# A three-stage transformer-like kernel: the lead-in's order of work rewritten, the third tile's scans and scores sooner, and a buffer of its own for the second tile's scores

## The chip, the cores and the metric

The kernel runs on one core of one Trainium2 chip. The metric is the device time of one execution in microseconds (us). The engines are called as the profile calls them: PE (TensorE matmuls; PEld its weight loads), DVE (VectorE), ACT (ScalarE), POOL (GpSimd) and SP (SyncE, which here only issues DMAs).

## The reference

Three stages follow each other. The first is a linear attention with a per-channel decay w over 4 batches, 8 heads of 48 channels and 768 positions:

```python
for t in range(S):
    cur = einsum('bhd,bhe->bhde', u[None] * kt, vt)
    y[:, :, t] = einsum('bhd,bhde->bhe', rt, state + cur)
    state = wt[:, :, :, None] * state + einsum('bhd,bhe->bhde', kt, vt)
```

The second is a dense layer pair on the 3072 tokens of 384 channels, with 2048 hidden units and a leaky slope alpha for each; the third sends each token to the one of 8 experts whose embedding it is nearest to:

```python
h = x @ w_in
x = (np.maximum(h, 0.0) + alpha * np.minimum(h, 0.0)) @ w_out
...
logits = normed(x) @ normed(expert_emb).T / tau
expert_idx = np.argmax(logits, axis=1)
out[mask] = gate_w[mask, None] * (np.maximum(x[mask] @ w1[e], 0.0) @ w2[e])
```

## The kernel before, in words

**Tiles and blocks.** The attention is cut into 24 tiles n of 128 tokens (six chunks of time by four batches); three tiles make a block j of the dense layers, and there are 8 blocks. The dense weights come in sixteen chunks, eight of w_in and eight of w_out in turn, each of 256 hidden units: SP loads a chunk into one of four staging buffers `stg` (`load_stage`, L185 and L187), and `conv` turns it into two single-precision parts in four steps c0 to c3: c0 on ACT (L196), c1 on DVE (L198 and L199, two instructions), c2 on ACT, which rounds the high part (L210, `win0h`, `wout0h`), c3 on DVE, which subtracts it for the low part (L212, `win0l`, `wout0l`). A chunk's c3 releases the staging buffer for the load four chunks on. The converted weights stay for all blocks, so chunks are converted only during the first block.

**The steps of a tile**, numbered as in the table of functions `ATT`: a0 `att_p0` (the first scan over w on DVE, L261, with L263 to L267), a1 `att_p1` (the second scan, L270), a2 `att_p2` (k transposed, copied by ACT at L322), a3 `att_p3` (the scores `a_ps`, L331, copied into `A` by ACT at L334 and masked there by two POOL selects, L335), a4 `att_p4` (the tile's result `y_ps`, L365, added to `dv` by DVE at L367), a5 `att_p5` (`y` transposed on PE and split into `xh` on ACT at L382 and `xl` on DVE at L383: what the dense layers read), a6 `att_r` (r and k scaled by the scans' result: on DVE at L286), a7 `att_d` (the diagonal term: `dg` L302, and `dv`, either by eight ACT copies at L305 or by one DVE product at L307), a8 `att_w` (L276 on ACT, the sums of the decays), a9 `att_s` (the state: `u_ps` L344, `st` L350). The state of a tile enters the results of the next chunk of time, four tiles on.

**The dense steps.** `l1(j, f)` computes one 128-unit slice f of block j's hidden layer: nine products of 384 columns into `h_ps` (L407), then ACT (L411) and DVE (L412) form the activation `m`; `l1_hi` and `l1_lo` split it (`gh` L421 on ACT, `gl` L426 on DVE). `l2(j, f)` adds the slice's nine products to the block's output `o_ps` (L436). `warm(n)` issues n idle products (L391) whose result nobody reads.

**What sets the order.** Each engine runs its instructions in the order in which the program issues them. The opening is the string `PLAN` (L78): "aQ.N" is step Q of tile N, "cQ.C" step Q of the conversion of chunk C, "l1.f" the slice f of block 0, "wN" N warm products, "p0.G" and "p1.G" a small product of an output-weight chunk with the expert embeddings, "s" and "e" those embeddings' norm (L890, L891) and transpose (L887), "g" the split of all waiting `m`. Behind it a loop over T issues, for each T: the attention steps 2 to 5 that are due, an early group of conversion steps, one slice of `l1`, the slice of `l2` two T back, a late group, the attention steps 0, 1, 6 and 8, and `l1_lo`. A tile's due times are a start (`START`, `AT1`, `AT`) plus lags (`LAGS`). A tile's load is issued once the steps that read the same buffer two tiles back are issued.

Where the diff speaks: `AD` (tiles n < AD form `dv` on ACT), `AT1` (starts of the tiles of blocks 1 and 2 within their block), the one buffer `A` of all tiles' scores, the pool `ps_a` from which `y_ps` is taken (three buffers, shared with `a_ps`, `kt_ps`, `u_ps` and `ep`), and the dictionary `sched` of the due steps.

## Time and profile before

| | us |
|---|---|
| median of 3 runs | 821.88 |
| lowest, highest | 821.51, 823.42 |
| the profiled execution: its own time | 818.76 |
| its span | 816.9 |
| PE busy in the span | 793.8 (97%) |
| DVE busy | 582.0 (71%) |
| ACT busy | 435.2 (53%) |
| POOL busy | 300.9 (37%) |

The profile cuts the span into 40 slices of 20.4 us. PE's slices, in tenths: 8 in the first slice, 8, 7 and 9 in the next ones (warm products among them), and 9 (90% or more) to the end but for two of 8 and the last of 7. The granted TensorE clock is full in all slices but the third (6 tenths of full speed, 40.8 to 61.3 us). Places in the trace are given in us from the span's start. The opening of `PLAN` takes the first 52 us or so; conversions on DVE and ACT go on until about 112 us; behind that the dense layers and the attention's tiles share the engines until the routed experts begin.

How to read it: a row of a timeline has the start, the duration, the engine, the line, the operation, and its operands; in brackets at the end is the time for which the engine had waited just before and what released it. Durations of neighbouring instructions of one engine overlap a little, so where a stretch is measured, start to start is meant.

### The profile page before, as it was taken

How to read it: one execution, taken by the hardware profiler on the slowest of the kernel's cores; microseconds unless marked ns; L12 is line 12 of the kernel's file. 1: busy time of each engine (PE TensorE's matmuls, PEld its weight loads, DVE VectorE, ACT ScalarE, POOL GpSimd, SP SyncE). 2: the span in 40 equal slices, each digit the busy share in tenths (PEclk: the TensorE clock that was granted, in tenths of full speed). 3: DMA queues.
4: the chain of work that ended last, by engine and by line, in shares of the span. 5: the costliest groups of instructions: out<-in, count | busy, mean ns of one | idle time of the engine just before them, and what ended most of it. 6: DMA issues, size and time to landing. Idle time of an engine off the chain costs nothing. (4 is left out here: it accounts for less than half of the span.)

```text
span 816.9 us, 16480 instructions
## 1 busy us (share of the span) xinstructions
PE 793.8 (97%) x6466; PEld 755.7 (93%) x6466; DVE 582.0 (71%) x1229; ACT 435.2 (53%) x861; POOL 300.9 (37%) x365
## 2 busy tenths in 40 slices
PE   8879999999999999999999999998999999999997
PEld 5669899999999999999999999898899999999997
DVE  7788967886686586676676774647987676767672
ACT  6667655435345435444534533436556676767662
POOL 2002222333223134124224212143466776767731
PEclk9969999999999999999999999999999999999999
DMA  9545520133424313113113100046756787686750
GB/s 322 167 156 197 183 75 2 69 118 117 156 84 139 131 33 102 66 63 99 69 70 98 69 1 31 31 169 205 193 198 211 273 278 254 218 285 211 263 187 33
DMA packets 31623, 114.86 MB, mean 141 GB/s; under 512 B 5756, under 2 KB 13148, under 8 KB 29232
## 3 DMA queue, kind: packets, MB, share of 16 engines
q0 software_dynamic: 13952, 59.86, 22.3%
q1 hardware_dynamic: 17584, 53.85, 19.5%
q8 instruction: 53, 0.87, 0.5%
q14 instruction: 34, 0.28, 0.2%
HBM read 99.36 MB, written 15.51 MB: 141 GB/s over the span
## 5 line engine op out<-in xcount | busy, mean ns | idle before, releaser
L411 ACT ACTIVATE m<-h_ps,al_sb 128x384 f32<-128x384 f32 x128 | 74.3, 581 | 139.4 <-PE h_ps L407 137.7
L412 DVE TENSOR_TENSOR m<-h_ps,m 128x384 f32<-128x384 f32 x128 | 71.0, 555 | 97.3 <-ACT m L411 96.6
L421 ACT ACTIVATE gh<-m 128x384 fp32r<-128x384 f32 x128 | 67.1, 525 | 111.1 <-DVE m L412 111.1
L335 POOL TENSOR_SCALAR_AFFINE_SELECT A<-A 128x512 f32<-128x512 f32 x48 | 32.9, 710 | 208.1 <-ACT A L334 208.1
L426 DVE TENSOR_TENSOR gl<-m,gh 128x384 fp32r<-128x384 f32 x128 | 81.3, 636 | 38.2 <-ACT gh L421 38.0
L689 POOL DMA_INDIRECT raw<-in_w,wix x64 | 67.4, 1054 | 48.6 <-DVE w0l L701 21.3
L731 PE MATMUL h_ps<-yh,w0h 128*128 128x256 f32 x264 | 77.4, 293 | 3.4 <-DVE g2l L736 3.4
L731 PE MATMUL h_ps<-yl,w0h 128*128 128x256 f32 x264 | 75.0, 284 | 0.3 <-DVE yl L722 0.3
L731 PE MATMUL h_ps<-yh,w0l 128*128 128x256 f32 x264 | 74.7, 283 | 0.0
L701 DVE TENSOR_TENSOR w1l<-raw,w1h 128x768 fp32r<-128x768 f32 x64 | 60.6, 953 | 19.8 <-ACT w1h L700 19.1
L407 PE MATMUL h_ps<-xh,win0h 128*128 128x384 f32 x192 | 69.2, 360 | 2.3 <-DVE m L412 1.5
L701 DVE TENSOR_TENSOR w0l<-raw,w0h 128x768 fp32r<-128x768 f32 x64 | 60.8, 959 | 12.5 <-ACT w0h L700 12.5
L407 PE MATMUL h_ps<-xh,win1h 128*128 128x384 f32 x192 | 68.0, 354 | 0.0
L436 PE MATMUL o_ps<-wout0h,gh 128*128 128x392 f32 x192 | 66.7, 347 | 0.0
L407 PE MATMUL h_ps<-xh,win0l 128*128 128x384 f32 x192 | 65.4, 341 | 1.1 <-DVE win0l L212 1.1
L436 PE MATMUL o_ps<-wout0l,gh 128*128 128x392 f32 x192 | 65.9, 343 | 0.0
L436 PE MATMUL o_ps<-wout0h,gl 128*128 128x392 f32 x192 | 65.9, 343 | 0.0
L436 PE MATMUL o_ps<-wout1h,gh 128*128 128x392 f32 x192 | 65.8, 343 | 0.0
L407 PE MATMUL h_ps<-xl,win0h 128*128 128x384 f32 x192 | 65.5, 341 | 0.1
L436 PE MATMUL o_ps<-wout1h,gl 128*128 128x392 f32 x192 | 65.3, 340 | 0.0
L436 PE MATMUL o_ps<-wout1l,gh 128*128 128x392 f32 x192 | 65.2, 340 | 0.0
L407 PE MATMUL h_ps<-xh,win1l 128*128 128x384 f32 x192 | 64.9, 338 | 0.0
(282 smaller groups left out, 2261.8 us busy)
## 6 DMA issues: line engine op xcount, KB each, us to landing
ld<-in_att SPq DMA_DIRECT2D x18, 1348.5 KB, 5.8
stg<-in_w_in SPq DMA_DIRECT2D x24, 256.0 KB, 3.9
stg<-in_w_out SPq DMA_DIRECT2D x8, 768.0 KB, 4.2
x2d<-rows SPq DMA_DIRECT2D x24, 194.0 KB, 7.3
out<-zero SPq DMA_DIRECT2D x24, 192.0 KB, 6.5
ld<-in_att SPq DMA_DIRECT2D x5, 512.0 KB, 5.2
ld<-in_att SPq DMA_DIRECT2D x3, 452.5 KB, 4.6
raw<-in_w,wix POOLq DMA_INDIRECT x64, 6.1
```

The costliest lines, as they stand in the source:

```text
L335: POOL.affine_select(out=h, in_=h, pattern=[[0, HP], [1, CH]], compare_op=ALU.is_gt, fill=0.0, base=0, channel_multiplier=-1)
L407: PE.matmul(out=h, lhsT=w[:, k, :], rhs=x[:, k, :], start=(n == 0), stop=(n == 3 * KD - 1))
L411: ACT.activation(out=m, in_=h, func=AF.Copy, scale=al_sb[:, f:f + 1])
L412: DVE.tensor_tensor(out=m, in0=h, in1=m, op=ALU.min)
L421: ACT.activation(out=gh, in_=m_t[j, f], func=AF.Copy)
L426: DVE.tensor_tensor(out=gl, in0=m_t.pop((j, f)), in1=gh.bitcast(F32), op=ALU.subtract)
L436: PE.matmul(out=o_t[j][i], lhsT=g[:, s], rhs=w, start=(f == 0 and n == 0), stop=(f == KF - 1 and n == 2))
L689: POOL.indirect_dma_start(out=t, out_offset=None, in_=src, in_offset=idx(wix[:, h, COL[s]:COL[s] + 1]))
L701: DVE.tensor_tensor(out=lo, in0=a, in1=hi.bitcast(F32), op=ALU.subtract)
L731: PE.matmul(out=h, lhsT=w[:, k, :], rhs=x[:, k, :], start=(n == 0), stop=(n == 3 * KD - 1))
```

## The change

`PLAN` is another string. Tile 2's scans and its `att_r` (a0.2, a1.2, a6.2) stand right behind tile 1's, ahead of a4.0; a3.1 and a3.2 stand sooner; l1.0 is preceded by fewer steps of chunk 1 (c2.1, c3.1 and the rest now follow it); "s", "e", a2.1, p0.0 stand behind l1.0; l2.0 and l2.1 are in the plan, the second as the last main product; the warm products in it are 11 where they were 38 (the 28 that open the program are left). Tile 1's scores get a buffer `A1` in the pool `rows`; `y_ps` of tiles 0 to 2 comes from `ps_o`. Tiles 3, 4 and 5 form `dv` on ACT. Tile 3 starts 2 T later, tile 4 1 T later, tile 5 as before. On SP, the load of chunk 4 stands now ahead of tile 3's load, where it stood behind, and tile 5's load stands behind ten chunk loads where it stood behind eight. Lines of the kernel behind L324 stand 3 to 6 later: L331 is now L334, L334 is L337, L365 is L369, L367 is L371, L382 and L383 are L386 and L387, L407 is L411, L411 is L415, L412 is L416, L426 is L430, L436 is L440.

```diff
--- before.py
+++ after.py
@@ -60,7 +60,7 @@
 STEP8 = 2
 HOLD = [1, 2, 1]
 ND = range(6)
-AD = 2
+AD = (0, 1, 3, 4, 5)
 WARM0 = 28
 WPD = (2, 3)
 EARLY = [(0, 0, -2), (0, 1, -2), (0, 2, -1), (0, 3, -1), (1, 0, 0), (1, 1, 0)]
@@ -75,9 +75,9 @@
 LAGS = [0, 1, 4, 4, 6, 7, 2]
 
 LOADS = [(0, "w"), (0, "rk"), "id", "v", (0, "n"), "e", (1, "w"), (1, "rk"), (1, "n"), (2, "w"), (2, "rk"), (2, "n"), 0, 1, 2, 3, "u"]
-PLAN = "a0.0 a1.0 a8.0 a2.0 w6 a6.0 a3.0 a7.0 w8 a0.1 a1.1 a6.1 s a4.0 a3.1 a9.0 a2.1 e c0.0 a7.1 a9.1 w8 a0.2 c0.1 c0.2 a1.2 a6.2 c1.0 a4.1 w8 a3.2 c1.1 a7.2 a5.0 a5.1 c2.0 w4 a4.2 p0.0 c3.0 a5.2 c2.1 c1.2 l1.0 c3.1 c2.2 l1.1 p1.0 c0.3 c3.2 g l1.2 w4 a8.1 a2.2 a9.2"
-
-AT1 = [0, 4, 8]
+PLAN = "a0.0 a1.0 a8.0 a2.0 w6 a6.0 a3.0 a7.0 a0.1 a1.1 a6.1 w5 a3.1 a0.2 a1.2 a6.2 a4.0 c0.0 a7.1 a4.1 a3.2 c1.0 c0.1 a7.2 a5.0 a5.1 c2.0 a4.2 c3.0 a5.2 a9.0 s c1.1 c0.2 l1.0 a2.1 c2.1 g p0.0 c3.1 e c1.2 l1.1 p1.0 c0.3 c2.2 g c3.2 l2.0 c1.3 l1.2 l2.1 a9.1"
+
+AT1 = {1: [2, 5, 8], 2: [0, 4, 8]}
 AT = {2: [-1, 6], 3: [-4, 1, 7]}
 NSG = 4
 WP = 1536
@@ -134,7 +134,7 @@
     R, P = (PS[:, HP * CW * i:HP * CW * (i + 1)].rearrange("p (h t) -> p h t", h=HP)[:, :, 2:CW] for i in range(2))
     R1 = PS[:, 3:3 + HP * CW].rearrange("p (h t) -> p h t", h=HP)[:, :, 0:CH]
     anew = cp.tile([128, LW], BF16, name="anew")
-    A = atp.tile([128, H, CH], F32, tag="at", name="A")
+    A0 = atp.tile([128, H, CH], F32, tag="at", name="A")
     st_all = atp.tile([128, B, HP, D], F32, tag="st", name="st")
     st = [st_all[:, b] for b in range(B)]
     sbd_all = atp.tile([128, 2, HP, 2 * D], F32, tag="st", name="sbd")
@@ -300,7 +300,7 @@
             v = nat(n, 2).rearrange("p (h d) -> p h d", h=H)
             dg = sp.tile([128, H, 1], F32, tag="dg", name="dg")
             ACT.activation(out=dg, in_=dp, func=AF.Copy)
-            if n < AD:
+            if n in AD:
                 for h in range(H):
                     ACT.activation(out=dv[:, h, :], in_=v[:, h, :], func=AF.Copy, scale=dg[:, h, :])
             else:
@@ -321,8 +321,11 @@
                 PE.transpose(kt[:, h, :], k[:, h, :], ident)
             ACT.activation(out=Kt, in_=kt, func=AF.Copy)
 
+    A_t = {}
+
     def att_p3(n):
 
+        A = A_t[n] = rp.tile([128, H, CH], F32, tag="rows", name="A1") if n == 1 else A0
         r, k = rT(n, 0), rT(n, 1)
         a = [ps_a.tile([128, HP, CH], F32, tag="a", name="a_ps") for _ in range(2)]
         for h in range(HP):
@@ -352,9 +355,10 @@
     def att_p4(n):
         c, b = divmod(n, B)
         r, v = rT(n, 0), nat(n, 2)
+        A = A_t.pop(n)
         if 0 < c < NCH - 1:
             att_s(n)
-        yp = ps_a.tile([128, DM], F32, tag="a", name="y_ps")
+        yp = ps_o.tile([128, DM], F32, tag="o", name="y_ps") if n < BT else ps_a.tile([128, DM], F32, tag="a", name="y_ps")
 
         for hp in range(HP):
             for q in (slice(0, 64), slice(64, 128)):
@@ -850,17 +854,19 @@
         sched = {}
         for n in range(NTILE):
             j = max(q for q in range(NB) if B0[q] <= n)
-            t0 = START[n] if j == 0 else 16 * (j - 1) + (AT1 if j < 3 else AT[BLK[j]])[n - B0[j]]
+            t0 = START[n] if j == 0 else 16 * (j - 1) + (AT1[j] if j < 3 else AT[BLK[j]])[n - B0[j]]
             for q, d in enumerate(LAGS0 if j == 0 else LAGS1 if j == 1 else LAGS):
                 sched.setdefault(t0 + d, []).append((q, n))
-            sched.setdefault(1 if n == 2 else t0 + 3, []).append((8, n))
+            sched.setdefault({1: 0, 2: 1}.get(n, t0 + 3), []).append((8, n))
+        sched.setdefault(1, []).append((2, 2))
+        sched.setdefault(2, []).append((9, 2))
 
         ran = set()
 
         def run(kind, *a):
             if (kind, *a) in ran:
                 return
-            if kind != "w":
+            if kind not in "wg":
                 ran.add((kind, *a))
             if kind == "a":
                 q, n = a
@@ -976,7 +982,7 @@
                     q = (T - 2) // 16
                     bg.append(chain(route(q), *((early_table(), early_loads()) if q == NB - 2 else (last_table(),) if q == NB - 1 else ())))
             convs(T, 1)
-            pieces(T, (0, 1, 6, 8))
+            pieces(T, (0, 1, 6, 8, 9))
             if j and (j, f) in m_t:
                 l1_lo(j, f)
             step(STEP7 if j >= NB - 1 else 1)
```

**DVE in the opening.** `att_129` holds tile 2's decays, `ld` a loaded tile's; `y` is a finished tile, `en_192` the embeddings' norm. Before, from the last step of tile 1 on:

```order
L286 TENSOR_TENSOR ld<-ld,PS 128x512
L890 TENSOR_SCALAR en_192<-en_192 8x1
L891 RECIPROCAL en_192<-en_192 8x1
L367 TENSOR_TENSOR y<-y_ps,dv 128x384
L261 SCALAR_TENSOR_TENSOR PS<-att_129,anew 128x520
L263 TENSOR_SCALAR ip_all<-PS 128x4
```

With the change, from the same place:

```order
L286 TENSOR_TENSOR ld<-ld,PS 128x512
L261 SCALAR_TENSOR_TENSOR PS<-att_129,anew 128x520
L263 TENSOR_SCALAR ip_all<-PS 128x4
L264 RECIPROCAL att_129<-ip_all 128x4
L266 TENSOR_TENSOR att_129<-att_129 128x512
L267 TENSOR_TENSOR att_129<-att_129,PS 128x512
L270 SCALAR_TENSOR_TENSOR PS<-att_129,anew 128x519
L286 TENSOR_TENSOR att_129<-att_129,PS 128x512
L371 TENSOR_TENSOR y<-y_ps,dv 128x384 x2
L198 SCALAR_TENSOR_TENSOR stg<-stg 128x768
L199 SCALAR_TENSOR_TENSOR stg<-stg 128x768
L307 TENSOR_TENSOR dv<-att_129,dg 128x384
```

Tile 2's seven steps follow tile 1's without a step between; the norm and the sum of tile 0's result, which stood ahead of them, come behind, and tile 0's and tile 1's sums follow each other.

**ACT in the opening.** `dv_403` and `dv_377` are the diagonal term of tile 1, `dg` its factors, `A_125` the shared buffer of scores, `A1_330` the new one. Before, with what each waits for:

```order
L196 ACTIVATE stg_163<-stg_163 128x768 [waits DMAHW6_49,DMAHW5_49,DMAHW4_49]
L302 ACTIVATE dg_404<-dg_ps_398 128x8 [waits PE_49]
L305 ACTIVATE dv_403<-ld_156,dg_404 128x48 [waits DMAHW0_49,DVE_49,Activation_49]
L305 ACTIVATE dv_403<-ld_156,dg_404 128x48 x7
L350 ACTIVATE st_126<-u_ps_414 48x192 [waits PE_49]
L350 ACTIVATE st_126<-u_ps_414 48x192
L196 ACTIVATE stg_167<-stg_167 128x768 [waits DMAHW7_49]
L196 ACTIVATE stg_169<-stg_169 128x768 [waits DMAHW2_49,DMAHW1_49,DMAHW0_49]
L334 ACTIVATE A_125<-a_ps_487 128x512 [waits PE_49,Pool_49]
L334 ACTIVATE A_125<-a_ps_488 128x512 [waits PE_49,Pool_49]
```

With the change:

```order
L337 ACTIVATE A1_330<-a_ps_331 128x512 [waits PE_49]
L337 ACTIVATE A1_330<-a_ps_332 128x512 [waits PE_49]
L196 ACTIVATE stg_163<-stg_163 128x768 [waits DMAHW6_49,DMAHW5_49,DMAHW4_49]
L302 ACTIVATE dg_378<-dg_ps_372 128x8 [waits PE_49]
L305 ACTIVATE dv_377<-ld_156,dg_378 128x48 [waits DMAHW0_49,DVE_49,Activation_49]
L305 ACTIVATE dv_377<-ld_156,dg_378 128x48 x7
L337 ACTIVATE A_125<-a_ps_407 128x512 [waits PE_49,Pool_49]
L337 ACTIVATE A_125<-a_ps_408 128x512 [waits PE_49,Pool_49]
```

Tile 1's scores are copied into their own buffer without a wait for POOL; the eight copies of tile 1's `dv`, whose first one waits for a DMA and for DVE as before, stand ahead of the copies of tile 2's scores.

**DVE around tile 5's first scan**, in the main loop; the line of `y` is tile 3's result, whose step also releases the buffer that tile 5's load fills; the scan is tile 5's. Before, two pieces, eight rows apart:

```order
L367 TENSOR_TENSOR y<-y_ps,dv 128x384
L198 SCALAR_TENSOR_TENSOR stg<-stg 128x768
L199 SCALAR_TENSOR_TENSOR stg<-stg 128x768
L412 TENSOR_TENSOR m<-h_ps,m 128x384
L212 SCALAR_TENSOR_TENSOR win1l<-stg,win1h 128x3x256
```

```order
L426 TENSOR_TENSOR gl<-m,gh 128x384
L198 SCALAR_TENSOR_TENSOR stg<-stg 128x768
L199 SCALAR_TENSOR_TENSOR stg<-stg 128x768
L412 TENSOR_TENSOR m<-h_ps,m 128x384
L212 SCALAR_TENSOR_TENSOR win1l<-stg,win1h 128x3x256
L261 SCALAR_TENSOR_TENSOR PS<-ld,anew 128x520
L263 TENSOR_SCALAR ip_all<-PS 128x4
```

With the change:

```order
L286 TENSOR_TENSOR ld<-ld,PS 128x512
L430 TENSOR_TENSOR gl<-m,gh 128x384
L371 TENSOR_TENSOR y<-y_ps,dv 128x384
L198 SCALAR_TENSOR_TENSOR stg<-stg 128x768
L199 SCALAR_TENSOR_TENSOR stg<-stg 128x768
L416 TENSOR_TENSOR m<-h_ps,m 128x384
L212 SCALAR_TENSOR_TENSOR win1l<-stg,win1h 128x3x256
L261 SCALAR_TENSOR_TENSOR PS<-ld,anew 128x520
L263 TENSOR_SCALAR ip_all<-PS 128x4
```

The scan stood 18 rows behind the sum of tile 3's result and stands 5 rows behind it; tile 5's `dv` (L307) is no longer on DVE.

## Rows read from the trace of the kernel before

**Rows 1.** The page's first part: busy time, share of the span, instructions.

```profile
PE 793.8 (97%) x6466; PEld 755.7 (93%) x6466; DVE 582.0 (71%) x1229; ACT 435.2 (53%) x861; POOL 300.9 (37%) x365
```

**Rows 2.** Windows: length, busy of PE, PEld, DVE, ACT, POOL; clock, DMA share, GB/s.

```profile
45.00:50.00 5.00, 3.00 (x56) 2.58 (x57) 4.83 (x9) 3.30 (x6) 0.00 (x0) 0.50 0.05 21
...
80.00:90.00 10.00, 10.00 (x125) 9.18 (x126) 9.19 (x14) 8.54 (x19) 2.56 (x3) 1.00 0.44 138
```

**Rows 3.** DVE's timeline from 60 to 130 us.

```profile
64.33 0.56 DVE L412 TENSOR_TENSOR m<-h_ps,m 128x384 f32<-128x384 f32 x1 [2.14 <-ACT m L411]
...
86.39 0.56 DVE L412 TENSOR_TENSOR m<-h_ps,m 128x384 f32<-128x384 f32 x1 [0.64 <-ACT m L411]
...
111.03 0.56 DVE L412 TENSOR_TENSOR m<-h_ps,m 128x384 f32<-128x384 f32 x1 [0.80 <-ACT m L411]
```

**Rows 4.** PE's timeline from 28 to 53 us.

```profile
28.72 1.14 PE L365 MATMUL y_ps<-att,A 128*64 128x48 f32 x32
...
31.88 0.44 PE L407 MATMUL h_ps<-xh,win0h 128*128 128x384 f32 x1 [0.78 <-ACT xh L382]
...
33.98 0.34 PE L407 MATMUL h_ps<-xh,win0h 128*128 128x384 f32 x1
...
35.66 0.59 PE L243 MATMUL wq_ps<-enT,wt 128*32 128x8 f32 x48
...
46.17 1.55 PE L232 MATMUL wt_ps<-ident,stg 128*128 128x128 f32 x6 [3.77 <-DVE stg L199]
...
49.37 0.70 PE L436 MATMUL o_ps<-wout0h,gh 128*128 128x392 f32 x1
...
52.48 0.85 PE L298 MATMUL dg_ps<-u_bd,ld 128*128 128x2 f32 x4
```

**Rows 5.** DVE's timeline in the opening: tile 1's, then tile 2's first and last step.

```profile
8.54 1.23 DVE L261 TENSOR_TENSOR_SCAN PS<-ld,anew 128x520 f32<-128x520 f32 x1
...
12.67 0.94 DVE L286 TENSOR_TENSOR ld<-ld,PS 128x512 f32<-128x512 f32 x1
...
15.78 1.23 DVE L261 TENSOR_TENSOR_SCAN PS<-att,anew 128x520 f32<-128x520 f32 x1
...
20.71 0.69 DVE L286 TENSOR_TENSOR att<-att,PS 128x512 f32<-128x512 f32 x1
```

**Rows 6.** ACT's timeline in the opening: tile 1's `dv`, tile 2's scores.

```profile
19.60 1.91 ACT L305 ACTIVATE dv<-ld,dg 128x48 f32<-128x48 f32 x8
...
26.40 1.09 ACT L334 ACTIVATE A<-a_ps 128x512 f32<-128x512 f32 x2 [2.58 <-PE a_ps L331]
```

**Rows 7.** DVE's timeline, 45 to 56 us: tile 3's scans and chunk 4.

```profile
46.03 1.24 DVE L261 TENSOR_TENSOR_SCAN PS<-ld,anew 128x520 f32<-128x520 f32 x1
...
48.91 0.95 DVE L198 SCALAR_TENSOR_TENSOR stg<-stg 128x768 int32<-128x768 int32 x1
...
51.64 1.23 DVE L270 TENSOR_TENSOR_SCAN PS<-ld,anew 128x519 f32<-128x519 f32 x1
...
54.63 0.95 DVE L212 SCALAR_TENSOR_TENSOR win0l<-stg,win0h 128x768 fp32r<-128x768 f32 x1
```

**Rows 8.** DVE's timeline, 73 to 79 us.

```profile
73.80 0.55 DVE L367 TENSOR_TENSOR y<-y_ps,dv 128x384 f32<-128x384 f32 x1
...
77.51 1.00 DVE L286 TENSOR_TENSOR ld<-ld,PS 128x512 f32<-128x512 f32 x1
78.43 0.55 DVE L307 TENSOR_TENSOR dv<-ld,dg 128x384 f32<-128x384 f32 x1
78.90 0.55 DVE L426 TENSOR_TENSOR gl<-m,gh 128x384 fp32r<-128x384 f32 x1
```

**Rows 9.** The page's part on DMA issues: count, size, us to landing.

```profile
ld<-in_att SPq DMA_DIRECT2D x5, 512.0 KB, 5.2
```

**Rows 10.** Windows of PE alone: length, busy; clock, DMA share, GB/s.

```profile
19.00:20.00 1.00, 1.00 (x19) 0.76 1.02 352
...
57.00:58.00 1.00, 1.00 (x9) 0.97 0.97 340
```

## The prediction

> **What bounds the kernel now.** The page's first part comes first: PE is busy for 97% of the span, no other engine for more than 71% [rows 1]. Behind the opening the kernel is therefore as long as PE's work, and what a change of the opening can give is the time at which PE's full stretch begins, plus what PE idles for in between. Next come the windows: from 45 to 50 us PE is busy for 3.00 of 5.00 us at half clock while DVE is busy for 4.83; from 80 to 90 us PE is full, but DVE is busy for 9.19 of 10 and ACT for 8.54 [rows 2]. The timeline of DVE shows what this means: between 60 us and the last conversion, just behind 111 us, DVE waits only three times for the activation of a dense product, 2.14, 0.64 and 0.80 us [rows 3]. So from 45 to about 112 us the conversion of the weights on DVE sets the pace; PE is handed a product when its converted weights are there, and its high busy share means that it is just able to follow. Last, PE's timeline of the opening: tile 2's result y2 starts at 28.72, the first main product l1.0 at 31.88, there is an idle stretch of 3.77 before 46.17 for a conversion on DVE, and l2.0 starts at 49.37 [rows 4].
>
> The reader is to take from this two different questions: how much sooner the first main product starts, and how much of that survives until DVE has done its list. The second decides.
>
> **How much sooner l1.0 starts.** Tile 1's seven steps on DVE last from 8.54 to 12.67 + 0.94 = 13.61, that is 5.07; tile 2's, the same seven, from 15.78 to 20.71 + 0.69 = 21.40, that is 5.62 [rows 5]. With the change they start at 13.61 and end, by the one or the other length, between 18.7 and 19.2; I take 19.0. The sum of tile 0's result follows on DVE (0.55 [rows 8]), to 19.5. Now ACT: the eight copies of tile 1's dv stand ahead of the copy of tile 2's scores, and the first of them waits for DVE; I read that wait as one for tile 0's sum, because dv's buffer is in use until then. The copies last 1.91 [rows 6], to 21.4. From the start of the scores' copy (26.40) to y2 (28.72) it was 2.32 [rows 4, 6]: y2 starts at 23.7, not 28.72. From y2 to l1.0 it was 3.16 at a mostly full clock [rows 4]; at half clock a third more is the most that I allow, 4.2. So l1.0 starts between 26.9 and 27.9 against 31.88: 4.0 to 4.9 us sooner, 4.4 taken.
>
> The tile's own buffer for scores does little of this. The copy of tile 1's scores no longer waits for tile 0's masked scores, but tile 2's copy, the one that y2 needs, stands behind dv anyway.
>
> **What survives.** I keep a ledger for DVE, the engine that sets the pace, up to the end of chunk 4's conversion (54.63 before [rows 7]).
>
> 1. *The lead, 4.4 at l1.0.* Some of it is lost at half clock: nine products took 1.68 us at full clock (33.98 to 35.66) and 3.11 at half (49.37 to 52.48) [rows 4], 1.43 more. If the clock comes back during the first products, one group's half is lost at most; I take a loss of 0.6, and the lead that reaches chunk 4 is 3.8 (bounds 2.6 and 4.9).
> 2. *Tile 3's scans, not yet done there.* Tile 3 starts two T later. Its first scan with the three steps behind it stood ahead of that place on DVE and took 46.03 to 48.91, 2.88; its second scan 51.64 to 52.78 in DVE's queue, about 1.15 [rows 7]. DVE still owes 4.0. Lead and debt together: +0.2 (bounds -0.9 and +1.4).
> 3. *Three products dv (tiles 3, 4, 5) leave DVE.* Start to start one takes 78.43 to 78.90, 0.47 [rows 8]: -1.4. They come back on ACT as 1.91 each [rows 6]; with ACT busy for 3.30 of 5 us from 45 to 50 [rows 2] I price that at nothing while DVE is the later of the two. If ACT's spare time is gone, it costs what the fourth case below says.
> 4. *The three waits of before* [rows 3], 3.6 in all, are in DVE's time of before and not forced by its list: -3.6 if PE is ahead by two groups, which l2.0 and l2.1 done in the opening give it.
> 5. *A new wait on DVE for tile 5's load.* Tile 5's first scan now stands five rows behind the sum of tile 3's result, whose step releases the load's buffer, and not eighteen. Those rows (the sum, two of a conversion, m, and the low part) took 73.80 to 77.51, 3.7 [rows 8]; the load lands 5.2 behind its issue [rows 9]. DVE waits for 1.5, and everything behind the scan on DVE with it: the l1 activations and the next conversions. Bounds: 0 if the release comes before the sum is through, 5.2 if nothing lies beside it. Taken +1.5.
> 6. *PE catches up.* DVE's list is now shorter by 5.0 (points 3 and 4), PE's is not, so some of the waits for products come back before 112 us: between 0 and the 3.6 of before; nearer the upper half, since PE was busy for all of 80 to 90 us [rows 2]. Taken +2.0.
>
> SP's order costs nothing by itself: the load of chunk 4 is now ahead of tile 3's, and tile 3 has two T more. Twenty-seven warm products fewer free no time, as PE waits wherever they stood; they matter through the clock only. The second accumulator pool for y0 to y2, and the norm of the embeddings standing later, are not on the path: their readers are the wprime products, which also come later.
>
> Sum: 0.2 - 1.4 - 3.6 + 1.5 + 2.0 = **-1.3 us**. Behind 112 us the instructions are the same, so that is the whole change. The profiled execution took 818.76 with a span of 816.9, 3.1 below the median of 821.88; the durations come from it, and only the difference is used: 821.88 - 1.3 = **820.6**. With the larger unknowns (points 1, 5, 6) not all on one side, the case's own range is 819.0 to 822.6. About 0.3%, or 2.5 us, is the least that a measurement of this kernel can tell from no change: 819.4 to 824.3 counts as the same.
>
> **The rivals.**
>
> *The clock stays full in the opening (faster).* Before, PE's granted clock fell in the window 19:20 (0.76) and was back in 57:58 (0.97), with l1.0 and l1.1 in between at full speed [rows 4, 10]. If the earlier scans keep PE fed from 19 us on, nothing of the lead is lost (4.9 against a debt of 4.0: -0.9 in place of +0.2), and PE, ahead by more, gives back only 0.8 of point 6: 820.6 - 1.1 - 1.2 = 818.3. Against it: the clock fell with 14 warm products ahead of it in the plan that the change takes out in part.
>
> *The clock stays at half through l2.1 (about the same).* Then l1.0 starts at 27.9, one to two groups of products cost 1.43 more [rows 4] on the way to chunk 4, and the lead that survives is 1.1 to 2.6, against the 3.8 that I took: +1.2 to +2.7, middle +2.0, which gives 822.6. For it speaks the fall at 19.5 [rows 10] and that fewer warm products follow. The Trainium skill, in "TensorE: Matmul & The Clock Gate", section "Part 1: The HAM clock gate (the "warmup" mystery)", says that "the default state is throttled, and activity releases the throttle"; by that rule a change which takes idle products away does so at the price of the clock, and the time would be this rival's 822.6. The trace agrees in part: the clock fell at 19 us, though warm products stood ahead.
>
> *DVE is not what sets the pace (faster).* If PE's products are what DVE's three waits show, and the rest only looks tight, a first product that starts 4.4 sooner is kept, less half a microsecond: 817.9. Against it: in 51 us DVE waits for a product for 3.6 [rows 3].
>
> *ACT becomes the bound (slower).* Three times eight copies, 1.91 each [rows 6], are put on ACT between T = 4 and T = 9, about 60 to 90 us, where it is busy for 8.54 of 10 us [rows 2]; each time gh and the next activation m stand behind the copies, and DVE and PE wait for these. The price is 5.7 less the 1.5 that is free there, 4.2: 820.6 + 4.2 = 824.8. It decides once ACT has no more than 1.9 us free in a T in which a dv stands ahead of m. For it: 8.54 of 10. Against it: from 90 us on, ACT's work per T must fall, for DVE is the busier of the two over the whole span [rows 1].
>
> *The change doesn't do what it says* in part: tile 2's scans come 2 us sooner, but the order on ACT (dv ahead of the scores) makes l1.0 wait, and nothing but the waits moves. That is 821.9; I count it with the first case, in whose range it lies.
>
> **How the numbers follow.** The forecast's case (DVE's list sets the pace and swallows the lead): 0.50. Clock full: 0.18. Clock at half: 0.13. ACT the bound: 0.10. DVE not the pace: 0.09. Faster than 819.4 are most of the second (0.15), the last (0.09) and the lower end of the first (0.06): 0.30. Slower than 824.3 are most of ACT's case (0.09) and what is left over of the half clock and of a late load of tile 5 (0.04): 0.13. The same: 0.57. The range leaves out the lower half of the two faster cases, 0.10, and most of ACT's, 0.10: 817.9 to 823.6.
>
> **What would show it.** In the changed kernel's profile tile 2's last step on DVE should end near 19, y2 start near 23.7 and l1.0 between 27 and 28. L212 of chunk 4 should end within 1 us of 54.6 less the 4.0 of tile 3's scans, and the last conversion near 111. If L261 of tile 5 waits for a DMA by more than 3 us, or an activation on ACT stands behind dv while DVE is idle, the fourth case or a late load is at work. If PE's granted clock from 27 to 42 us is full, the second case holds; if it is 0.5, the third. The prediction is wrong in its core if the last conversion ends 4 us sooner than before: then DVE's list did not swallow the lead.

## The result, and the profile after

The changed kernel takes 826.46 us (median of 5 runs, 825.88 to 826.62) against 821.88 of the kernel before measured beside it (5 runs): 1.0052 times, 95% interval [1.0037, 1.0067]. It is slower, by 4.6 us; the forecast was 820.6 in a range of 817.9 to 823.6. The profiled execution of the changed kernel took 826.46 with a span of 824.4, that of before 818.76 with 816.9; of these 7.5 us of span about 3 arise before 115 us, which this part is about, and the rest behind 550 us, which the last section takes up.

The page's first part, to be held against [rows 1]: no engine has more work, PE's is spread over a longer span.

```profile
PE 793.0 (96%) x6439; PEld 757.4 (92%) x6439; DVE 581.7 (71%) x1226; ACT 439.5 (53%) x885; POOL 301.2 (37%) x365
```

PE's clock in the opening: length and busy time of PE, then the granted clock, DMA share and GB/s.

```profile
19.00:26.00 7.00, 6.28 (x46) 0.54 0.38 129
26.00:32.00 6.00, 5.25 (x49) 0.50 0.31 77
32.00:38.00 6.00, 5.46 (x75) 0.90 0.66 228
```

The granted clock lies at half (its lower level, 1.2 GHz) from about 20 to 33 us, right where the first main products now run. PE's timeline of the opening answers to [rows 4]:

```profile
24.87 2.22 PE L369 MATMUL y_ps<-att,A 128*64 128x48 f32 x32
...
28.65 0.88 PE L347 MATMUL u_ps<-ld,Kt 128*48 128x48 f32 x16
29.46 0.69 PE L411 MATMUL h_ps<-xh,win0h 128*128 128x384 f32 x1
...
34.48 0.44 PE L411 MATMUL h_ps<-xh,win0h 128*128 128x384 f32 x1
...
39.65 0.44 PE L411 MATMUL h_ps<-xh,win0h 128*128 128x384 f32 x1 [0.16 <-ACT win0h L210]
...
50.63 0.89 PE L243 MATMUL wq_ps<-enT,wt 128*32 128x8 f32 x48 [4.20 <-ACT wt L234]
...
52.26 0.69 PE L411 MATMUL h_ps<-xh,win0h 128*128 128x384 f32 x1
```

Tile 2's result y2 starts at 24.87 (28.72 before), the first main product l1.0 at 29.46 (31.88): 2.4 us sooner, not 4.4. In front of l1.0 a state product u_ps has moved in. The next slices are not sooner: l1.1 starts at 34.48 (33.98 before) and l1.2 at 39.65, where the kernel before had

```profile
36.22 0.41 PE L407 MATMUL h_ps<-xh,win0h 128*128 128x384 f32 x1
```

Then PE idles 4.20 us before 50.63, for ACT, in the place of the 3.77 for DVE of before. The next rows are DVE's, to be held against [rows 3, 7]:

```profile
46.41 0.56 DVE L430 TENSOR_TENSOR gl<-m,gh 128x384 fp32r<-128x384 f32 x1 [2.17 <-ACT gh L425]
...
52.41 0.96 DVE L212 SCALAR_TENSOR_TENSOR win0l<-stg,win0h 128x768 fp32r<-128x768 f32 x1 [0.25 <-ACT win0h L210]
...
87.61 1.24 DVE L261 TENSOR_TENSOR_SCAN PS<-ld,anew 128x520 f32<-128x520 f32 x1 [2.27 <-DMA ld<-in_att]
...
110.14 0.56 DVE L416 TENSOR_TENSOR m<-h_ps,m 128x384 f32<-128x384 f32 x1 [1.46 <-ACT m L415]
...
113.98 0.56 DVE L416 TENSOR_TENSOR m<-h_ps,m 128x384 f32<-128x384 f32 x1 [1.95 <-ACT m L415]
114.46 0.95 DVE L212 SCALAR_TENSOR_TENSOR wout1l<-stg,wout1h 128x768 fp32r<-128x768 f32 x1
```

Chunk 4's low part (52.41, first line of L212) comes 2.2 us sooner than before (54.63), with tile 3's scans still to do. The runs below show that these 2.2 us are not the opening's. Later DVE waits 2.27 for tile 5's load, and twice for an activation, 1.46 and 1.95. The last conversion starts at 114.46; in the kernel before it started at 111.51. From there on the two kernels stay 2.9 us apart for the next 430 us. The loss is therefore made between 52 and 114 us. PE's first products of l1.8 and l1.12 narrow it down, before and after:

```profile
81.65 0.44 PE L407 MATMUL h_ps<-xh,win1h 128*128 128x384 f32 x1
...
104.60 0.44 PE L407 MATMUL h_ps<-xh,win1h 128*128 128x384 f32 x1
```

```profile
79.60 0.44 PE L411 MATMUL h_ps<-xh,win1h 128*128 128x384 f32 x1
...
107.57 0.44 PE L411 MATMUL h_ps<-xh,win1h 128*128 128x384 f32 x1
```

At l1.8 the changed kernel is 2.0 us ahead, though it still owes more of the tiles' later steps, and at l1.12 it is 3.0 behind. All engines from 60 to 110 us, before and after (length; busy of PE, PEld, DVE, ACT, POOL; clock, DMA share, GB/s):

```profile
60.00:110.00 50.00, 48.79 (x624) 44.74 (x625) 46.66 (x68) 35.57 (x73) 11.89 (x15) 1.00 0.48 159
```

```profile
60.00:110.00 50.00, 44.56 (x559) 41.29 (x559) 45.78 (x65) 39.28 (x95) 11.18 (x14) 1.00 0.48 159
```

At full clock in both, PE is busy for 48.79 of 50 us before and for 44.56 after: 4.2 us of idle time. DVE is busy for only 0.9 less. The waits of PE that are new are small and many; the clearest are the two in front of the scores a_ps of tiles 4 and 5:

```profile
83.61 0.49 PE L385 MATMUL t_ps<-ident,y 128*128 128x128 f32 x3
83.94 0.60 PE L321 MATMUL kt_ps<-ident,ld 128*128 128x128 f32 x4
84.47 0.48 PE L334 MATMUL a_ps<-ld 64*128 64x128 f32 x2
86.07 1.16 PE L334 MATMUL a_ps<-ld 64*128 64x128 f32 x14 [1.12 <-ACT Kt L322]
...
106.49 1.16 PE L334 MATMUL a_ps<-ld 64*128 64x128 f32 x14 [0.99 <-ACT Kt L322]
```

The transposes t_ps, kt_ps and the two halves of a_ps follow each other, and all four come from one pool, `ps_a`, with three accumulator buffers (in the kernel t_ps, wt_ps, wq_ps and dg_ps are taken from it too, which the list of its users ahead of the prediction leaves out). The first product into the fourth of them, with which the row of 14 begins, has to wait until t_ps or kt_ps has been read. It starts at 86.07, as Kt has just read kt_ps (85.43 + 0.58); t_ps is held longer, for xl reads it on DVE at 91.53. ACT shows why Kt is late:

```profile
84.65 0.51 ACT L425 ACTIVATE gh<-m 128x384 fp32r<-128x384 f32 x1
85.06 0.47 ACT L386 ACTIVATE xh<-t_ps 128x384 fp32r<-128x384 f32 x1
85.43 0.58 ACT L322 ACTIVATE Kt<-kt_ps 128x512 f32<-128x512 f32 x1
87.11 1.09 ACT L337 ACTIVATE A<-a_ps 128x512 f32<-128x512 f32 x2 [1.10 <-PE a_ps L334]
```

xh (L386), which reads t_ps, and Kt (L322), which reads kt_ps, stand behind gh in ACT's queue; the scores' own copy (L337) then waits 1.10 for PE. This is a stall that neither the sum nor a rival had.

### The profile page after: what moved, and what is told of

Its sections match the earlier page's. It is cut to its first block, busy times and chain, and to the rows that moved or that the text cites. A ratio compares the mean times of both kernels' runs of the same rounds, so it can differ in the third digit from the quotient of the medians.

```text
span 824.4 us, 16446 instructions
## 1 busy us (share of the span) xinstructions
PE 793.0 (96%) x6439; PEld 757.4 (92%) x6439; DVE 581.7 (71%) x1226; ACT 439.5 (53%) x885; POOL 301.2 (37%) x365
## 4 chain that ended last, share of the span: by engine, by line
PE 79%; DVE 8%; issue 5%; ACT 5%; POOL 1%; DMA 0%; POOLq 0%; SPq 0%; ACTq 0%; DVEq 0%
PE h_ps L411 23%; PE o_ps L440 22%; PE h_ps L735 9%; PE o_ps L761 8%; PE a_ps L334 3%; PE y_ps L369 2%; PE o_ps L793 2%; PE h_ps L771 2%; PE y_ps L366 2%; PE idle L395 1%; PE u_ps L347 1%; PE t_ps L385 1%; DVE w0l L705 1%; PE kt_ps L321 1%; DVE w1l L705 1%
## 5 line engine op out<-in xcount | busy, mean ns | idle before, releaser
L415 ACT ACTIVATE m<-h_ps,al_sb 128x384 f32<-128x384 f32 x128 | 74.3, 580 | 145.6 <-PE h_ps L411 135.6
L416 DVE TENSOR_TENSOR m<-h_ps,m 128x384 f32<-128x384 f32 x128 | 71.0, 555 | 101.8 <-ACT m L415 100.7
L430 DVE TENSOR_TENSOR gl<-m,gh 128x384 fp32r<-128x384 f32 x128 | 81.7, 639 | 39.4 <-ACT gh L425 37.5
L735 PE MATMUL h_ps<-yh,w0h 128*128 128x256 f32 x264 | 77.3, 293 | 3.2 <-DVE g2l L740 3.1
L411 PE MATMUL h_ps<-xh,win0h 128*128 128x384 f32 x192 | 70.1, 365 | 1.7 <-DVE m L416 1.5
L411 PE MATMUL h_ps<-xh,win1h 128*128 128x384 f32 x192 | 68.1, 355 | 1.7 <-DVE m L416 1.7
L411 PE MATMUL h_ps<-xh,win0l 128*128 128x384 f32 x192 | 66.0, 344 | 1.3 <-DVE win0l L212 1.3
L440 PE MATMUL o_ps<-wout0h,gh 128*128 128x392 f32 x192 | 66.0, 344 | 0.5 <-ACT wout0h L248 0.5
L411 PE MATMUL h_ps<-xl,win0h 128*128 128x384 f32 x192 | 66.2, 345 | 0.0
L440 PE MATMUL o_ps<-wout1h,gh 128*128 128x392 f32 x192 | 65.8, 343 | 0.1
L440 PE MATMUL o_ps<-wout1h,gl 128*128 128x392 f32 x192 | 65.5, 341 | 0.0
L440 PE MATMUL o_ps<-wout0l,gh 128*128 128x392 f32 x192 | 65.5, 341 | 0.0
L440 PE MATMUL o_ps<-wout0h,gl 128*128 128x392 f32 x192 | 65.3, 340 | 0.0
L440 PE MATMUL o_ps<-wout1l,gh 128*128 128x392 f32 x192 | 65.2, 340 | 0.0
L411 PE MATMUL h_ps<-xh,win1l 128*128 128x384 f32 x192 | 64.9, 338 | 0.0
```

Of the source, the lines that this page charges most:

```text
L411: PE.matmul(out=h, lhsT=w[:, k, :], rhs=x[:, k, :], start=(n == 0), stop=(n == 3 * KD - 1))
L415: ACT.activation(out=m, in_=h, func=AF.Copy, scale=al_sb[:, f:f + 1])
L416: DVE.tensor_tensor(out=m, in0=h, in1=m, op=ALU.min)
L430: DVE.tensor_tensor(out=gl, in0=m_t.pop((j, f)), in1=gh.bitcast(F32), op=ALU.subtract)
L440: PE.matmul(out=o_t[j][i], lhsT=g[:, s], rhs=w, start=(f == 0 and n == 0), stop=(f == KF - 1 and n == 2))
L735: PE.matmul(out=h, lhsT=w[:, k, :], rhs=x[:, k, :], start=(n == 0), stop=(n == 3 * KD - 1))
```

## The experiments

Times of the kernel before differ from chip to chip (medians of 819.5 to 823.9), so ratios to the kernel before on the same chip are compared. Beside them stands the start of the last conversion on DVE in the one profiled execution: 111.51 before, 114.46 after.

| run | ratio, 95% interval | last conversion |
|---|---|---|
| the change | 1.0052 [1.0037, 1.0067] | 114.46 |
| the change again (e15) | 1.0054 [1.0038, 1.0070] | 113.84 |
| e1 dv back on DVE | 1.0064 [1.0045, 1.0083] | 115.32 |
| e2 starts as before | 1.0008 [0.9995, 1.0020] | 111.00 |
| e3 the opening alone | 1.0016 [0.9998, 1.0035] | 111.78 |
| e4 the loop's parts alone | 1.0062 [1.0044, 1.0080] | 113.32 |
| e5 tile 5's scans later | 1.0046 [1.0030, 1.0061] | 113.90 |
| e6 tile 3 alone early | 1.0018 [1.0008, 1.0027] | 111.58 |
| e7 before, dv on ACT | 1.0001 [0.9986, 1.0017] | 111.47 |
| e8 before again | one run | 110.24 |
| e9 transposes later | 1.0033 [1.0016, 1.0049] | 114.38 |
| e10 before, transposes later | 1.0062 [1.0036, 1.0088] | 115.07 |
| e11 warm products back | 1.0032 [1.0016, 1.0048] | 112.94 |
| e12 e5 and e9 together | 1.0009 [0.9998, 1.0020] | 110.00 |
| e13 e2 and e11 together | 0.9992 [0.9978, 1.0005] | 110.51 |
| e14 e2 with the shared buffer | 1.0016 [1.0000, 1.0031] | 113.20 |
| e16 e12 and e11 together | 0.9991 [0.9981, 1.0001] | 109.56 |
| e17 old opening, e12's loop | 0.9998 [0.9987, 1.0009] | 110.38 |

Two executions of one program differ in the last column too: by 1.3 (before and e8) and 0.6 (the change and e15). Differences under about 1.3 us are not read from it alone, and a lead over the kernel before is taken against both of its executions, 111.51 and 110.24.

**Which part costs.** Four kernels, each with a part of the change undone or alone.

e1:
```diff
-AD = (0, 1, 3, 4, 5)
+AD = (0, 1)
```


> The changed kernel with one part undone: the diagonal term dv of tiles 3, 4 and 5 is formed by one DVE product again instead of by eight ACT copies (1.92 us a tile). Theory A (ACT is late in the main loop: PE's waits for Kt, wt and s_wp from 60 to 110 us, 3.6 us, stand behind these copies): 3 us below the changed kernel's 826.5, so 823 to 824. Theory B (the late start of tiles 3 and 4 costs, DVE waits for tile 5's load) and theory C (the new opening itself is slow, through the half clock from 20 to 33 us): within 1 us of 826.5, or up to 1.4 slower, since three products of 0.47 us go back to DVE.

e2:
```diff
-AT1 = {1: [2, 5, 8], 2: [0, 4, 8]}
+AT1 = {1: [0, 4, 8], 2: [0, 4, 8]}
```


> The changed kernel with one part undone: tiles 3 and 4 start 2 and 1 T sooner, as before. Theory B: the wait of 2.3 us for tile 5's load goes, and tile 3's scans fill the time in which DVE waits between 32 and 48 us: 2 to 3 us below 826.5, so 823.5 to 824.5. Theory A and theory C: within 1 us of 826.5.

e3 has both of these edits. 

> Only the new opening (order of the lead-in, own buffer for the second tile's scores, other pool for the first results): dv of tiles 3 to 5 on DVE and the starts of tiles 3 and 4 as in the kernel before. Theory C: still 3 us or more slower than the kernel before, 825 or above. Theories A and B: the first product 2.4 us sooner is kept in part, 819 to 822.

e4, in the kernel before (the two lines that read these are adapted as in the change):
```diff
-AD = 2
+AD = (0, 1, 3, 4, 5)
-AT1 = [0, 4, 8]
+AT1 = {1: [2, 5, 8], 2: [0, 4, 8]}
```


> The kernel before with only the two parts of the main loop: dv of tiles 3 to 5 on ACT, and tiles 3 and 4 starting 2 and 1 T later. The opening is that of before. Theories A and B: slower than before by 3 us or more, 825 or above. Theory C: within 1.5 us of before, 820.5 to 823.5.

Theory A falls: with dv back on DVE the kernel is no faster (1.0064). Theory C falls for the most part: the opening alone is within reach of no change. Theory B holds: with the starts of tiles 3 and 4 as before, 1.0008 and not 1.0052; and the loop's parts alone, under the old opening, cost the whole (1.0062).

These runs also show what the opening gives at chunk 4. Its low part on DVE, in e3 and in e4:

```profile
55.93 0.95 DVE L212 SCALAR_TENSOR_TENSOR win0l<-stg,win0h 128x768 fp32r<-128x768 f32 x1
```

```profile
49.17 0.95 DVE L212 SCALAR_TENSOR_TENSOR win0l<-stg,win0h 128x768 fp32r<-128x768 f32 x1
```

With tile 3's start as before it comes at 55.93 (e3), 55.65 (e2) and 54.62 (e6) under the new opening, and between 53.73 and 54.81 under the old one (before, e7, e8, e10). With the late starts it comes at 52.41 and 51.74 (the change, e15) under the new opening, and at 49.17 (e4) and 50.76 (e17) under the old one. So the new opening does not bring chunk 4 sooner, in most of these traces about 1 us later, although l1.0 starts 2.4 us sooner in it. The 2.2 us that the change is ahead at chunk 4 come from tile 3's scans, 4.0 us, which no longer stand in front.

**Which tile, and what of it.** The change with one edit each:

e5:
```diff
-                sched.setdefault(t0 + d, []).append((q, n))
+                sched.setdefault(t0 + d + (n == 5 and q < 2), []).append((q, n))
```


> The changed kernel with tile 5's two scans one T later, everything else as in the change; its load has then one T more to land. Theory B1 (what costs is DVE's wait of 2.3 us for that load, where it is later than the engine): the wait goes, 1.5 to 2.5 us below the changed kernel, ratio to before 1.002 to 1.004. Theory B2 (what costs is that tile 3's two scans and their three steps, 4.0 us, stand in the stretch where DVE has no time to spare, and no longer in the opening's): the wait goes, yet the time stays within 1 us of the changed kernel, ratio 1.004 to 1.007, as the other tiles' work lies just as tight.

e6: `AT1 = {1: [0, 5, 8], 2: [0, 4, 8]}`. 

> The changed kernel with tile 3 alone starting at T = 0 again; tile 4 stays 1 T later. Theory B2, and B1 too (tile 3 then frees tile 5's buffer 2 T sooner): as with both starts undone, ratio to before 1.000 to 1.002. If tile 4's later start is what costs: within 1 us of the changed kernel, ratio 1.004 or more.

e7, in the kernel before: `AD = (0, 1, 3, 4, 5)`. 

> The kernel before with one part alone: dv of tiles 3 to 5 on ACT. Two pairs of runs with the other parts equal differ by 0.9 and 0.8 us at the end of the conversions in favour of ACT. If that holds with the old opening and the old starts too, 0.5 to 1.4 us faster than before, ratio 0.998 to 0.9995. By the rival of the prediction that ACT becomes the bound: slower than before, ratio above 1.002.

e8 is the kernel before, unchanged. 

> The kernel before once more, unchanged. Its profiled execution was 3.1 us below its median, and the changed kernel's trace has an idle stretch of ACT of 6.6 us near 551 us that the trace of before lacks, after which the two stand 3.3 us further apart. If such a stretch belongs to any execution and not to the change, it stands here in the same place and the span is 818 to 822; if it belongs to the change, it is missing again and the span is 816 to 818.

Tile 3's start makes most of it (1.0018 with tile 3 early). dv on ACT is worth nothing that a measurement shows (1.0001). e5 took DVE's wait for the load away, and the time stayed within the intervals: DVE waits 7.4 us for activations m between 30 and 117 us where the changed kernel had 5.3, and of PE's two waits for a buffer the second grew from 0.99 to 1.77 us:

```profile
85.81 1.16 PE L334 MATMUL a_ps<-ld 64*128 64x128 f32 x14 [1.10 <-ACT Kt L322]
...
105.93 1.16 PE L334 MATMUL a_ps<-ld 64*128 64x128 f32 x14 [1.77 <-ACT Kt L322]
```

At this point theory B2, the mere amount of DVE's work in the full stretch, fitted everything. The next pair was made against it. e8's span of 817.3 has no stretch as the changed kernel had near 551 us (last section).

**The four accumulators in one T.** One edit, put into the change (e9) and into the kernel before (e10). Tiles that start three T apart bring the transposes of one tile and kt_ps and a_ps of the next into the same T; four T apart they are in neighbouring ones. The edit parts them in the change, and brings them together in the kernel before:
```diff
-                sched.setdefault(t0 + d, []).append((q, n))
+                sched.setdefault(t0 + d + (n in (3, 4) and q == 5), []).append((q, n))
```


> The changed kernel with one edit: the transposes of tile 3's and tile 4's result (t_ps, read by xh on ACT and xl on DVE) come one T later, so that they no longer stand in the same T as the next tile's kt_ps and a_ps; the four share three accumulator buffers. Theory B3 (the starts three T apart bring these four together, and PE idles for a buffer: 1.12 and 0.99 us in front of a_ps): these two waits go, 1.5 to 2.5 us below the changed kernel, ratio to before 1.002 to 1.004. Theory B2 (the amount of DVE work in the full stretch): no gain, ratio 1.004 or more.

> The kernel before with the same one edit: there it brings the transposes into the T of the next tile's kt_ps and a_ps, where they were not. Nothing is added to any engine. Theory B3: two waits of about 1 us in front of a_ps appear on PE, 1.5 to 2.5 us slower than before, ratio 1.002 to 1.003. Theory B2: ratio within 0.999 to 1.001.

In the kernel before the edit makes the stall, with no work added to any engine, and larger than expected, 1.0062. PE, then ACT, around the first of the two:

```profile
81.15 1.16 PE L331 MATMUL a_ps<-ld 64*128 64x128 f32 x14 [2.33 <-ACT Kt L322]
...
105.59 1.28 PE L331 MATMUL a_ps<-ld 64*128 64x128 f32 x14 [1.75 <-ACT Kt L322]
```

```profile
79.71 0.52 ACT L421 ACTIVATE gh<-m 128x384 fp32r<-128x384 f32 x1 [1.04 <-DVE m L412]
80.14 0.47 ACT L382 ACTIVATE xh<-t_ps 128x384 fp32r<-128x384 f32 x1
80.51 0.59 ACT L322 ACTIVATE Kt<-kt_ps 128x512 f32<-128x512 f32 x1
```

xh (L382) stands behind gh, gh waits 1.04 for m on DVE, and m stands there behind a conversion: t_ps, complete at 77.3, is read from 80.14 on, and PE idles 2.33 us for Kt, the next in ACT's queue. In the change the opposite edit took the two waits in front of a_ps away, and the last conversion did not move (114.38): DVE's wait for tile 5's load rose from 2.27 to 3.39, and PE waited 2.97 for an xl that stands on DVE twelve rows behind that scan. DVE's row, then PE's:

```profile
89.10 1.24 DVE L261 TENSOR_TENSOR_SCAN PS<-ld,anew 128x520 f32<-128x520 f32 x1 [3.39 <-DMA ld<-in_att]
```

```profile
97.92 0.56 PE L347 MATMUL u_ps<-ld,Kt 128*48 128x48 f32 x16 [2.97 <-DVE xl L387]
```

The ratio of e9, 1.0033, lies where theory B3 had it and B2 had not; its interval overlaps with the change's, so a gain of up to 2 us is neither shown nor excluded. So there are two stalls, each behind the other. e11 put the clock to the test:
```diff
-... a7.1 a4.1 a3.2 c1.0 c0.1 a7.2 ...
+... a7.1 w4 a4.1 w6 a3.2 c1.0 c0.1 w6 a7.2 ...
```


> The changed kernel with 16 warm products put back into the plan around tile 1's result, tile 2's scores and its diagonal term (4, 6 and 6), where PE idles or runs small products from 16 to 24 us. Theory C (the half clock from 20 to 33 us costs): the granted clock stays full or is back before 28 us, l1.0 starts 1 to 2 us sooner and 1 to 2 us are gained, ratio 1.003 to 1.004. Rival: the clock changes but the end does not, as behind 33 us the conversions set the start of the third product: ratio 1.005 to 1.006.

The granted clock then stays full until 26 us (length and busy time of PE, clock, DMA share, GB/s):

```profile
19.00:26.00 7.00, 5.78 (x62) 1.00 0.38 129
26.00:32.00 6.00, 5.12 (x52) 0.72 0.36 110
```

One execution without the warm products is not enough to hold against it, for the clock of the opening varies: in the nine runs with this opening, tile 1's own buffer and no added warm products it was 0.50 to 0.92 from 19 to 26 us (0.91 in e15), and l1.0 started between 29.34 and 29.68 in all of them. In the three runs with them (e11, e13, e16) it was 1.00, and l1.0 started at 29.02, 28.84 and 28.37. So the warm products do hold the clock, and bring l1.0 0.3 to 1.3 us sooner. The last conversion is 1.5 us sooner than in the change and 0.9 sooner than in e15; 1.0032 against 1.0052 have overlapping intervals, so a gain of about 1 us is possible and not shown.

**Both at once.** e12 has the edits of e5 and e9 together; tiles 3 and 4 still start late.


> The changed kernel with both single edits together: tile 5's two scans one T later and the transposes of tiles 3 and 4 one T later; tiles 3 and 4 still start late. Alone, the first took DVE's wait for the load away and the end came 0.6 us sooner, the second took PE's two waits for a buffer away and the end came 0.1 sooner, as each time the other one grew. Theory B4 (two stalls of the late starts cover each other: the load that lands late, and the four accumulators in one T): with both gone 2 to 3.5 us below the changed kernel, ratio to before 0.999 to 1.002. Theory B2 (the amount of DVE work in the full stretch): ratio 1.004 or more.

e15 is the change again, on the same chip. 

> The changed kernel once more, unchanged, for comparison with the run with both edits on the same chip: ratio to before 1.004 to 1.007, and the same two stalls in its trace.

1.0009 against 1.0054, and 3.8 us between the last conversions (110.00 and 113.84). Theory B4 holds and B2 falls, for the starts are as late as in the change. DVE has the same list: from chunk 4's low part to the last conversion, start to start and less its waits, it takes 56.5 us in e12 and 56.4 in the change (53.3 before). Its waits there are 1.7 us in e12, 5.7 in the change and in e15 (3.6 before, 2.0 in e8). Tile 5's scan follows the conversion without a wait (DVE's rows), and PE is busy for 47.26 of the 50 us. The change is 0.6 us behind e12 at l1.8 (79.60 against 79.04) and 4.8 behind at l1.12 (107.57 against 102.77), so it loses the time where the two stalls are:

```profile
88.19 0.56 DVE L416 TENSOR_TENSOR m<-h_ps,m 128x384 f32<-128x384 f32 x1 [0.74 <-ACT m L415]
88.66 0.95 DVE L212 SCALAR_TENSOR_TENSOR wout1l<-stg,wout1h 128x768 fp32r<-128x768 f32 x1
89.53 1.23 DVE L261 TENSOR_TENSOR_SCAN PS<-ld,anew 128x520 f32<-128x520 f32 x1
...
109.52 0.56 DVE L416 TENSOR_TENSOR m<-h_ps,m 128x384 f32<-128x384 f32 x1 [0.93 <-ACT m L415]
```

```profile
60.00:110.00 50.00, 47.26 (x580) 44.07 (x580) 47.67 (x70) 41.44 (x102) 12.74 (x15) 1.00 0.48 159
```

```profile
79.04 0.44 PE L411 MATMUL h_ps<-xh,win1h 128*128 128x384 f32 x1
...
102.77 0.45 PE L411 MATMUL h_ps<-xh,win1h 128*128 128x384 f32 x1
```

e13 joins e2 and e11, e16 joins e12 and e11, e17 has e12's two edits and the loop's parts under the old opening. e14 is e2 with the line of the own buffer taken back; there tile 1's scores overwrite tile 0's before tile 0's result is formed, so that result comes from tile 1's scores.

> The changed kernel with tiles 3 and 4 starting as before and the 16 warm products put back. If the two gains add (the early starts stood 3.5 us sooner at the end of the conversions, the warm products 1.5 us), the end of the conversions comes 2 us sooner than in the kernel before: ratio 0.997 to 0.999. If the clock's gain is swallowed here, ratio 1.000 to 1.001.

> The changed kernel with tiles 3 and 4 starting as before, and the own buffer for tile 1's scores taken back (all tiles share one). As the prediction said, the own buffer does little: within 0.7 us of the run with the early starts, ratio 1.000 to 1.002. If it matters, tile 1's copy waits until tile 0's result is through, and l1.0 starts 1 us or more later: ratio 1.002 or more.

> The changed kernel with both stalls removed (tile 5's scans and the transposes of tiles 3 and 4 one T later) and the 16 warm products put back. If the clock's gain of 1 to 1.5 us comes on top of the 1.5 us by which the run with both edits led the kernel before at the end of the conversions: ratio 0.996 to 0.999, faster than both kernels. If it is swallowed: ratio 0.999 to 1.001.

> The opening of the kernel before with the late starts and dv on ACT, and both stalls removed. If the late starts are good once the two stalls are gone, whatever the opening: ratio 0.997 to 0.9995. If they are good only behind the new opening, in which tile 3's scans would be in the way: ratio 1.000 to 1.002.

e13, e16 and e17 are level with the kernel before. Their last conversions (110.51, 109.56, 110.38) are 1.0 to 2.0 us ahead of the 111.51 and from 0.7 ahead to 0.3 behind the 110.24 of its two executions, so no lead over it is shown there either. e16 (0.9991 [0.9981, 1.0001]) beats the changed kernel clearly and the kernel before not certainly. e14's l1.0 starts at 32.63 where e2's starts at 29.39, and its last conversion is 2.2 us later: in this order of steps the own buffer is what makes l1.0 early (e14's tile 0 also has to wait for tile 1's scores, so a shared buffer in another order is not measured by it). The time differs by less than the intervals (1.0016 and 1.0008).

## Why the prediction was wrong, point by point

- *"So l1.0 starts between 26.9 and 27.9"*: 29.46. (By its own terms 26.86, so 5.0 us sooner at most and not 4.9; nothing hangs on it.) DVE's part was right (tile 2's last step ends at 19.58, 19.0 predicted; dv's copies waited for tile 0's sum, as read). y2 came at 24.87 instead of 23.7, took 2.22 us at half clock where [rows 4] had 1.14, and u_ps (0.88) stood in front of l1.0; the prediction counted no step that had moved in there.
- *"The tile's own buffer for scores does little of this"*: wrong for this order of steps. Without it l1.0 is 3.2 us later (e14).
- *Point 1, a lead of 3.8 that reaches chunk 4*: none did. The lead was gone by l1.1 (34.48 against 33.98), and with the opening alone (e3) chunk 4's low part comes 1.3 us later than before. Half clock is 1.1 of it (l1.0 lasts 3.16 us where it lasted 2.10); between l1.0 and l1.1 stand now kt_ps, wt_ps and ep, and l2.0 stands ahead of l1.2.
- *Point 2, a debt of 4.0*: right, 2.88 and 1.15 in the change too. In the change the two together were not +0.2 but 1.8 (4.0 owed, 2.2 ahead at chunk 4).
- *Point 3, -1.4 for dv, and ACT as the slower-side rival*: DVE's list is 1.4 shorter (the change against e1), but e7 shows no gain and no loss in time. In traces of pairs that differ in dv alone (the change and e1; e2 and e3) ACT's version stands 0.9 and 0.8 sooner, which is within what single executions differ by.
- *Points 4 and 6, three waits of 3.6 gone, 2.0 back*: 3.4 are back. PE had l2.0 and l2.1 done by 44.6 us and was 2.0 ahead at l1.8; the waits behind 80 us took this away.
- *Point 5, +1.5 for tile 5's load*: 2.27, somewhat more than predicted. e5 shows no gain beyond the intervals from taking it away alone.
- **The step that failed** is in points 1, 4 and 6. In the terms of its sum, up to the last conversion of the two profiled executions: the place at chunk 4 was forecast as -3.8 and is -2.2; DVE's waits behind it were forecast as 3.5 for the 3.6 of before (2.0 for products, 1.5 for the load), and are 5.7; debt and dv came as forecast, and 0.5 is instructions that ran longer. -2.2 + 4.0 - 1.4 + 2.1 + 0.5 gives 3.0, against 2.95 measured. The waits were mis-sized because PE was said to be ahead: the prediction looked at what each engine has to do, and not at which steps of two tiles fall into one T once the starts are three T apart. There the transposes and the next tile's scores ask for four of three accumulators, and PE idles behind ACT's queue. Estimated from the ratios, the late load alone (e9) costs 2.0 us over e12, this stall alone (e5) 3.0, and both together (e15) 3.7, each give or take about 1.5: less than the two added. With both gone DVE waits for 1.7.
- *"from 45 to about 112 us the conversion of the weights on DVE sets the pace"*: half right. PE was busy for 48.79 of the 50 us from 60 to 110. Both engines had little slack, so a stall of either could go to the end.
- *The clock as read from the kernel before*, fallen in 19:20 and back in 57:58, was two falls and not one. It was back at 23 us and fell again at 43, when PE stood idle:

```profile
23.00:24.00 1.00, 1.00 (x25) 1.00 0.68 166
...
43.00:44.00 1.00, 0.00 (x0) 0.71 1.02 362
```

- *The clock at half through l2.1*: it came in part, at half from 20 to 33 us, through l1.0 but not through l2.1, with a price in the opening and none that the total shows. The Trainium skill, in "TensorE: Matmul & The Clock Gate", section "Part 1: The HAM clock gate (the "warmup" mystery)", has activity release the throttle; by that rule warm products should bring the clock back, and the traces agree: 1.00 from 19 to 26 us in the three runs with 16 of them, 0.50 to 0.92 in the nine without.
- The sign had 0.13 for slower than 824.3. Most of it (0.09) was for ACT as the bound, which e1 and e7 do not bear out; the late load, which had a part of the other 0.04, is one of the two stalls. The other, the four accumulators, stood in no case.

## What to carry to other kernels

When the starts of overlapping pipelines are shifted, write down for each step of the loop which stages of two neighbours now fall together, and count the buffers of every shared pool there: a schedule can be worse with the same work on every engine. Where two engines are both full, a stall may hide a second one of the same size; removing either alone may show little, so test both together before calling either innocent. A lead at the first product is not a lead of the opening; here 2.4 us sooner at l1.0 was gone by l1.1.

## What the runs showed that was not expected

In the changed kernel's profile ACT stands still for 6.59 us at a place that has nothing to do with the change, though the product that it names as its releaser had, by PE's rows, been followed by others long before:

```profile
557.34 0.58 ACT L415 ACTIVATE m<-h_ps,al_sb 128x384 f32<-128x384 f32 x1 [6.59 <-PE o_ps L440]
```

It costs 3.3 us there. Such stretches, of 2.6 to 6.8 us, stand near the same place in all of e1 to e4 and e9 to e11, and in none of e5 to e8 and e12 to e17, the change again (e15) and the kernel before (e8) among them. The kernel before, measured beside the first set, has medians of 822.9 and 823.9, beside the second 819.8, 819.7 and 819.5. So it goes with the chip on which a set of runs was made, as far as one trace of each shows, and not with the change. What ACT waits for there was not found. It also means that the 7.5 us between the two spans shown first are not all the change's: its own part is about the 2.9 at the last conversion, and the medians (4.6 us apart beside the first profile, 3.7 with e15) say that better than a pair of spans.
